# The last row of w_down in two loads, of 88 and of 40 partitions

## The chip, the cores and the metric

One core of a Trainium2 chip runs the kernel. The metric is device time in microseconds (us) of one execution. Most executions agree within 0.3%. With five or six executions the 95% intervals below reach about 0.13% to each side, which is 0.24 us, so a difference of 0.1 us can't be told from the times.

## The reference

A decode step for two rows: an adaLN modulation, an attention over a window of the key and value caches, and a gated feed-forward layer. Only its end matters here:

```python
def _B_ref(x, w_gate, w_up, w_down):
    return _gelu(x @ w_gate) * (x @ w_up) @ w_down
...
h = _layernorm(x, axis=-1) * (1 + cb) + sb
x = x + gb * _B_ref(h, B_w_gate, B_w_up, B_w_down)      # w_down is 1536 x 640, bf16
```

## The kernel before

The kernel is a stream of loads. One queue (SP) brings 77 MB of weights and caches into one large tile, `arena`; the engines work on each part as it lands. Each of the 128 partitions gets 12 consecutive rows of `w_down`, and these 12 "rows" (one row is 640 elements, 1280 B, in each partition) come in three loads: rows 0 to 7, rows 8 to 10, and row 11 alone. The last load is small so that little work is left when the last byte is in.

```python
WD_SPLIT = [(0, 8), (8, 3), (11, 1)]
...
sem_of = {it: S.sem("d_%s" % "_".join(str(z) for z in it)) for it in place}   # a semaphore for each load
...
        return B_w_down.rearrange("(p r) n -> p (r n)", r=FC)[:, r0 * D:(r0 + nr) * D]
...
def pump(*consumed):
    ...
        queue["ops"][it] = S.dma("sp", k_dma(view(it), source(it)), sem_of[it], writes=keys(it), ...)
...
for ci, (r0, nr) in enumerate(WD_SPLIT):
    def f(e, r0=r0, nr=nr):
        for fc in range(r0, r0 + nr):                 # four matmuls for each row
            wv = wd_v[:, fc, :].rearrange("p (i n) -> p i n", i=NR)
            for i in range(NR):
                last = e.matmul(ps[32 * i:32 * i + RM, BK_OT, CY:CY + DR], lhsT=aT[:, fc, :], rhs=wv[:, i, :], ...)
        return last
    S.op("pe", f, reads=["aT"] + keys(("wd", ci)), writes=[bank(BK_OT)], name="down%d" % ci)
# then two DVE operations (fin, finb) and the store of the result
```

A load's semaphore gets 16 increments in all. Where a load runs on 16 DMA engines, each engine adds one when its share has landed, so the landing of a load is the landing of its slowest engine.

## Time and profile before

| | before |
|---|---|
| time, median of 6 runs | 186.06 us (185.94 to 186.15) |
| share of 16 DMA engines' span filled by the SP queue | 96.9% |
| rows 0 to 7: landed, matmuls start | 180.52, 180.65 us |
| rows 8 to 10: landed, matmuls start | 181.65, 181.70 us |
| row 11: landed, matmuls start | 182.05, 182.09 us |

The landings are the last of a load's 16 semaphore increments in the trace; the matmul starts are from the timeline.

Part 3 of the page of the kernel before gives, for each DMA queue, its packets, the megabytes and the share of 16 engines' span that its packets took. The loads fill the machine.

```profile
q1 hardware_dynamic: 2604, 76.88, 96.9%
q8 instruction: 5, 0.08, 0.2%
```

The end of the chain of waits of the kernel before (start, duration, what; in us), followed back from the last instruction. The 26 us of DMA are not 26 us of work on w_down: the load was issued early and stood behind others. What it says is that the last matmuls wait for w_down.

```profile
155.58 26.07 DMA arena<-in_B_w_down_dram
181.65 0.04 issue
181.70 0.39 PE ps L706 x12
182.08 0.01 issue
182.09 0.28 PE ps L706 x4
182.37 0.02 issue
182.39 0.34 DVE fin L711
```

The timeline of the kernel before over the same stretch (start, duration, engine, line, operation, output and inputs, count, and in brackets the idle time ahead and what ended it). The three groups of weight loads (PEld) of line 706 are the three loads' rows: 32 matmuls, 12 and 4.

```profile
180.63 0.54 PEld L706 LDWEIGHTS ps<-arena,aT 128*17 128x17 bf16 x32 [0.38 <-DVE aT L697]
...
181.69 0.18 PEld L706 LDWEIGHTS ps<-arena,aT 128*17 128x17 bf16 x12 [0.52 <-DMA arena<-in_B_w_down_dram]
...
182.09 0.10 PEld L706 LDWEIGHTS ps<-arena,aT 128*17 128x17 bf16 x4 [0.21 <-DMA arena<-in_B_w_down_dram]
182.39 0.33 DVE L711 TENSOR_TENSOR fin<-ps,modR 128x160 f32<-128x160 f32 x1 [1.81 <-PE ps L706]
```

Quarter-microsecond windows of the kernel before. The columns after the window's length are the busy times of PE, PEld, DVE, ACT and POOL with counts, then PE's clock, the mean busy share of the 16 DMA engines, and GB/s. The share falls from 0.96 to 0.49 at 179.50 and then needs two microseconds to reach zero: the engines end one after another.

```profile
179.25:179.50 0.25, 0.11 (x2) 0.00 (x0) 0.01 (x1) 0.00 (x0) 0.00 (x0) 1.00 0.96 374
179.50:179.75 0.25, 0.00 (x0) 0.00 (x0) 0.25 (x1) 0.00 (x0) 0.00 (x0) 1.00 0.49 190
179.75:180.00 0.25, 0.00 (x0) 0.00 (x0) 0.25 (x1) 0.00 (x0) 0.00 (x0) 1.00 0.53 210
...
181.00:181.25 0.25, 0.25 (x24) 0.17 (x12) 0.00 (x0) 0.00 (x0) 0.00 (x0) 1.00 0.21 77
181.25:181.50 0.25, 0.14 (x8) 0.00 (x0) 0.00 (x0) 0.00 (x0) 0.00 (x0) 1.00 0.10 36
181.50:181.75 0.25, 0.05 (x4) 0.06 (x8) 0.00 (x0) 0.00 (x0) 0.00 (x0) 1.00 0.02 5
```

The trace also holds every DMA packet with its start, duration, size and queue, but not its engine, and no view prints them one by one. A packet starts where the one before it on its engine ends, so the packets can be chained into 16 engines. Where the text below speaks of an engine's packets, it is from such chains. The engine that ended last ran its last packet at 181.51 us; the first engine was done with everything at about 179.45. The five engines that end more than 1.4 us behind the first are the five that carried one packet of the instruction queue each (16 KB, 0.94 to 1.07 us long, at 36, 97, 135, 162 and 177 us). Each such packet left its engine about 1.5 us behind: about 1 us is the packet itself, and the data packet right behind it took about 0.5 us longer than others of its size (at 178 us, 880 ns where 385 is usual). Nothing later gave that back, since every engine has an equal share of every load. A sixth engine, with an 8 KB packet at 89 us, is 1.0 us behind. In what follows these six are the late engines.

### The profile page before, as it was taken

The page shows a single profiled execution, that of the slowest core. Times are in us where ns is not written, and L with a number is a line of the kernel's source. Part 1 is how long each engine was busy: PE and PEld are TensorE (multiplying, and loading weights), DVE is VectorE, ACT ScalarE, POOL GpSimd, SP SyncE. Part 2 cuts the span into 40 slices and gives each one's busy share as a digit, 9 for nine tenths or more (in the row PEclk, how much of TensorE's full clock was granted, in tenths as well). Part 3 has the DMA queues.
Part 4 walks back from the last instruction along what each step waited for, and adds up shares of the span by engine and source line. Part 5 has one row for each costly group of instructions (what it writes and reads, how often), then busy time and mean ns, then how long its engine had stood idle before and what let it go on. Part 6 is the DMA issues. An engine that isn't in the chain of part 4 may idle for free.

```text
span 184.9 us, 1610 instructions
## 1 busy us (share of the span) xinstructions
PE 104.3 (56%) x843; PEld 26.1 (14%) x552; DVE 106.8 (58%) x97; ACT 14.5 (8%) x28; POOL 6.7 (4%) x29
## 2 busy tenths in 40 slices
PE   0015400937666096662598667748663299866853
PEld 0011000020000000001360002400000266411211
DVE  6213000039996489965994999387995649302311
ACT  2032100060000000001000000100000100220410
POOL 7700000000000000000000000000000000000000
PEclk9999999996999759998599999987999669999999
DMA  9999998999897999999898989899999989899980
GB/s 349 433 495 425 425 425 362 429 425 495 367 511 340 511 404 447 457 394 479 374 479 365 500 351 500 383 468 436 425 450 394 491 367 486 378 388 435 419 365 28
DMA packets 2626, 76.97 MB, mean 416 GB/s; under 512 B 314, under 2 KB 444, under 8 KB 572
## 3 DMA queue, kind: packets, MB, share of 16 engines
q1 hardware_dynamic: 2604, 76.88, 96.9%
q8 instruction: 5, 0.08, 0.2%
q14 instruction: 1, 0.01, 0.0%
q10 hardware_dynamic: 16, 0.01, 0.0%
HBM read 76.88 MB, written 0.00 MB: 416 GB/s over the span
## 4 chain that ended last, share of the span: by engine, by line
DMA 57%; DVE 22%; PE 17%; ACT 1%; issue 1%; SPq 0%
DMA arena<-in_A_k_cache_dram 36%; DMA arena<-in_B_w_down_dram 14%; DVE arena L518 12%; DMA arena<-in_w_mod_dram 8%; PE ps L581 8%; DVE S_sb L537 6%; PE ps L530 5%; DVE Em L567 2%; PE ps L470 2%; DVE negm L547 1%; ACT E_sb L555 1%; PE ps L558 1%; DVE M L543 0%; PE ps L551 0%; SPq L287 0%
## 5 line engine op out<-in xcount | busy, mean ns | idle before, releaser
L530 PE MATMUL ps<-arena,ident_b 128*128 128x512 bf16 x192 | 50.7, 411 | 30.2 <-DVE arena L518 30.1
L518 DVE TENSOR_TENSOR arena<-arena,qbc 128x3072 bf16<-128x3072 bf16 x32 | 54.8, 1749 | 11.1 <-DMA arena<-in_A_k_cache_dram 11.1
L581 PE MATMUL ps<-arena,Em 128*64 128x384 bf16 x256 | 24.5, 357 | 5.6 <-DVE Em L567 5.6
L537 DVE TENSOR_REDUCE S_sb<-ps 128x32 f32<-128x1024 f32 x16 | 19.5, 1219 | 8.4 <-PE ps L530 8.4
L581 PEld LDWEIGHTS ps<-arena,Em 128*64 128x64 bf16 x256 | 15.4, 121 | 29.8 <-DVE Em L567 22.2
L567 DVE TENSOR_TENSOR Em<-E_sb,maskE 128x2048 bf16<-128x2048 bf16 x8 | 18.0, 2282 | 2.6 <-PE ps L581 2.6
L492 PE MATMUL ps<-arena,hT 128*2 128x512 bf16 x60 | 4.7, 485 | 11.7 <-DMA arena<-in_A_wq_dram 11.7
L502 DVE CAST qrow<-ps 128x512 bf16<-128x512 f32 x1 | 0.7, 693 | 15.6 <-PE ps L492 15.6
L545 PEld LDWEIGHTS ps<-ident_f,M 128*1 128x1 f32 x2 | 0.2, 80 | 61.5 <-DVE M L543 61.5
L555 ACT ACTIVATE E_sb<-S_sb,nbias 128x256 bf16<-128x256 f32 x2 | 1.0, 507 | 69.3 <-DVE nbias L553 69.3
L651 DVE COPY arena<-ps 128x320 f32<-128x320 f32 x1 | 0.5, 491 | 10.1 <-PE ps L643 10.1
L643 PE MATMUL ps<-arena,oT 128*2 128x320 bf16 x96 | 3.9, 299 | 2.4 <-DMA arena<-in_A_wo_dram 2.4
L588 ACT ACTIVATE On<-ps,rden 128x384 bf16<-128x384 f32 x2 | 1.2, 582 | 47.5 <-PE ps L581 47.5
L403 PE MATMUL ps<-ident_b,crow 2*128 2x2 bf16 x5 | 0.4, 177 | 7.9 <-POOL zsel L383 7.9
L678 PE MATMUL ps<-arena,h2T 128*2 128x384 bf16 x40 | 3.8, 455 | 1.7 <-DMA arena<-in_B_w_up_dram 1.4
L470 PE MATMUL ps<-arena,scT 128*17 128x480 bf16 x40 | 4.3, 597 | 0.5 <-DMA arena<-in_w_mod_dram 0.5
L415 PE MATMUL ps<-Em,ident_b 128*128 128x512 bf16 x17 | 4.2, 379 | 0.2 <-issue 0.2
L408 DVE CAST X<-xr 128x160 f32<-128x160 bf16 x1 | 0.2, 244 | 6.1 <-DMA xr<-in_A_x_dram 6.1
L687 DVE TENSOR_TENSOR aR<-ps,gl 128x384 bf16<-128x384 f32 x1 | 0.6, 558 | 5.4 <-PE ps L678 5.4
L424 PE MATMUL ps<-st,selstat 128*128 128x2 f32 x4 | 0.9, 298 | 4.9 <-ACT sqj L420 4.9
L478 DVE TENSOR_SCALAR opc<-modR 128x160 f32<-128x160 f32 x2 | 0.5, 245 | 5.1 <-ACT modR L475 5.1
L492 PEld LDWEIGHTS ps<-arena,hT 128*2 128x2 bf16 x20 | 0.6, 100 | 15.8 <-issue 15.8
(89 smaller groups left out, 52.6 us busy)
## 6 DMA issues: line engine op xcount, KB each, us to landing
arena<-in_A_v_cache_dram SPq DMA_DIRECT2D x4, 6144.0 KB, 27.2
arena<-in_A_k_cache_dram SPq DMA_DIRECT2D x3, 6144.0 KB, 36.0
arena<-in_A_wq_dram SPq DMA_DIRECT2D x1, 7680.0 KB, 31.3
arena<-in_A_wo_dram SPq DMA_DIRECT2D x1, 6240.0 KB, 27.0
arena<-in_A_k_cache_dram SPq DMA_DIRECT2D x2, 3072.0 KB, 42.7
arena<-in_w_mod_dram SPq DMA_DIRECT2D x1, 4800.0 KB, 14.0
arena<-in_B_w_gate_dram SPq DMA_DIRECT2D x1, 1920.0 KB, 20.7
arena<-in_B_w_up_dram SPq DMA_DIRECT2D x1, 1920.0 KB, 22.7
```

Source lines behind the costliest of these rows:

```text
L415: last = e.matmul(ps[:, BK_T, :], lhsT=ident_b[:, :], rhs=Em[:, 0, 0:512 // H, :].rearrange("p j h -> p (j h)"), start=True, stop=True)
L470: last = e.matmul(ps[32 * i:32 * i + RM, half, 0:MH].rearrange("p (m n) -> p m n", n=DR), lhsT=scT[:, k, :], rhs=wv[:, 3 * half:3 * half + ...
L492: last = e.matmul(ps[32 * i:32 * i + B, n, :], lhsT=hT[:, k, :], rhs=wv[:, kk, i, n * QW:(n + 1) * QW], start=(k == 0), stop=(k == KT - 1) ...
L518: S.op("dve", lambda e: e.tensor_tensor(out=kt, in0=kt, in1=qbc[:, b, :].unsqueeze(1).broadcast_to([P, JC, Dh]), op=ALU.mult), reads=[("qb ...
L530: last = e.matmul(o_ap, lhsT=ident_b[:, :], rhs=kt[:, :, t * GC:(t + 1) * GC], start=(t == 0), stop=(t == NCH - 1))
L537: S.op("dve", lambda e: e.tensor_reduce(out=S_sb[:, b, 2 * JC * pair:2 * JC * (pair + 1)], in_=ps[:, 2 * z:2 * z + 2, :].rearrange("p k (j ...
L547: S.op("dve", lambda e: e.tensor_reduce(out=negm[:, b, :].rearrange("p (h x) -> p h x", x=XQ), in_=ps[0:1, BK_T, 0:P].rearrange("p (h x) - ...
L555: S.op("act", lambda e: e.activation(out=E_sb[:, b, :], in_=S_sb[:, b, :], func=ACTF.Exp, scale=SCALE, bias=nbias[:, b:b + 1], accum_out=d ...
L567: S.op("dve", lambda e, z=z, j=j: e.tensor_tensor(out=Em[:, z, :, :], in0=E_sb[:, b, j:j + JE].unsqueeze(2).broadcast_to([P, JE, H]), in1= ...
L581: last = e.matmul(ps[64 * i:64 * i + 2 * H, BK_O, 0:ON], lhsT=Em[:, z, 2 * jp:2 * jp + 2, :].rearrange("p j h -> p (j h)"), rhs=view(it, l ...
L643: last = e.matmul(ps[32 * i:32 * i + B, bk, 0:w], lhsT=oT[:, t, :], rhs=wv[:, tl, lo:lo + w], start=(t < NR), stop=(t >= NT - NR), tile_po ...
L678: last = e.matmul(ps[32 * i:32 * i + B, bk, 0:FT].rearrange("p (m r) -> p m r", r=FR), lhsT=h2T[:, k, :], rhs=wk[:, i, :, :], start=(k == ...
```

## The change

The intent: row 11 should not be put on the engines that end late. A load of 88 partitions and a load of 40 partitions use 11 and 10 of the 16 DMA engines, so that five engines carry nothing of the last row. Each of the two loads has its own semaphore, and the last four matmuls wait for both.

```diff
         sem_c = S.sem("d_c")
-        sem_of = {it: S.sem("d_%s" % "_".join(str(z) for z in it)) for it in place}
+        LAST = ("wd", len(WD_SPLIT) - 1)
+        LAST_SPLIT = [(0, 88), (88, P)]
+        sem_of = {it: S.sem("d_%s" % "_".join(str(z) for z in it)) for it in place if it != LAST}
+        sem_last = [S.sem("d_last%d" % n) for n in range(len(LAST_SPLIT))]
...
-                queue["ops"][it] = S.dma("sp", k_dma(view(it), source(it)), sem_of[it], writes=keys(it), ...)
+                if it == LAST:
+                    for n, (p0, p1) in enumerate(LAST_SPLIT):
+                        S.dma("sp", k_dma(view(it)[p0:p1, :], source(it)[p0:p1, :]), sem_last[n], writes=keys(it) if n == 0 else [("last", n)], ...)
+                else:
+                    queue["ops"][it] = S.dma("sp", k_dma(view(it), source(it)), sem_of[it], writes=keys(it), ...)
...
-            S.op("pe", f, reads=["aT"] + keys(("wd", ci)), writes=[bank(BK_OT)], name="down%d" % ci)
+            S.op("pe", f, reads=["aT"] + keys(("wd", ci)) + ([("last", n) for n in range(1, len(LAST_SPLIT))] if ("wd", ci) == LAST else []), ...)
```

More of the change, by code (lines that the diff above doesn't have):

```diff
@@ L336, in pump @@
                     break
-                queue["ops"][it] = S.dma("sp", k_dma(view(it), source(it)), sem_of[it], writes=keys(it), name="ld_%s" % "_".join(str(z) for z in it))
+                if it == LAST:
+                    for n, (p0, p1) in enumerate(LAST_SPLIT):
+                        S.dma("sp", k_dma(view(it)[p0:p1, :], source(it)[p0:p1, :]), sem_last[n], writes=keys(it) if n == 0 else [("last", n)], name="ld_last%d" % n)
+                else:
+                    queue["ops"][it] = S.dma("sp", k_dma(view(it), source(it)), sem_of[it], writes=keys(it), name="ld_%s" % "_".join(str(z) for z in it))
                 queue["next"] += 1
@@ L708, in f @@
                 return last
-            S.op("pe", f, reads=["aT"] + keys(("wd", ci)), writes=[bank(BK_OT)], name="down%d" % ci)
+            S.op("pe", f, reads=["aT"] + keys(("wd", ci)) + ([("last", n) for n in range(1, len(LAST_SPLIT))] if ("wd", ci) == LAST else []), writes=[bank(BK_OT)], name="down%d" % ci)
         S.op("dve", lambda e: e.tensor_tensor(out=fin[:, :], in0=ps[:, BK_OT, CY:CY + DR], in1=modR[:, 5, :], op=ALU.mult),
```

## The prediction

> **What bounds the kernel now.** Its loads: the page's third part has the SP queue's packets filling 96.9% of 16 engines' span. The chain of waits is 57% DMA; its last stretch is 26.07 us of w_down loading (155.58 to 181.65), then the final matmuls, two DVE operations and the store. The last row (160 KB) is the last load.
>
> **How the loads end.** In quarter-microsecond windows the DMA share is about 0.96 until 179.50, then 0.49, 0.53, 0.40, 0.36, 0.33, 0.29, 0.21, 0.10, 0.02: the engines do not end together. I chained the trace's packet records end to start. The fastest engine ends the last row at 179.45, eleven engines within 1.0 us of it, five at +1.5 to +2.1 us, the slowest at 181.56. Each of the five carried one 16 KB instruction fetch (at 36, 97, 135, 162, 177 us), which put it about 1.5 us behind. This gives no engine numbers. Each engine carries 8 packets of the last row, one every 52 ns: 0.41 us.
>
> **What the last row costs.** In the timeline the matmuls of rows 0 to 7 start at 180.65, those of rows 8 to 10 at 181.70 (load landed 181.66), those of row 11 at 182.09 (landed 182.05). A row takes four matmuls, 0.07 us, so row 11 could have issued at about 181.92. Its own exposed wait is only 0.17 us. Rows 8 to 10 arrive as late as before on the slowest engine; that 0.5 us wait isn't touched.
>
> **What the change does.** The Trainium skill, "DMA: Bandwidth & Descriptors", section "Why a DMA increments its semaphore by 16 and not by 1", says the engine count is the largest number up to 16 that divides the outer dimension, and that the lowest-numbered engines are used; no run here shows it yet. Then engines 0 to 9 carry 8 + 4 packets (0.62 us, +0.21), engine 10 carries 8, engines 11 to 15 none. It adds one issue on SP (0.44 us, 26 us early: free) and a second semaphore ahead of row 11's matmuls (the same double wait takes a 51 ns instruction at 180.54; hidden if both landed).
>
> - The five late engines are 11 to 15, as the choice of 88 and 40 suggests: the last row lands near 181.2, before rows 8 to 10; row 11 follows at once: -0.12 to -0.17 us. Chance 0.6.
> - The slowest is skipped but another late one isn't: landing near 182.05, nothing won, perhaps +0.05. 0.2.
> - The slowest is among 0 to 9: landing at 182.26, +0.2 to +0.3 us. 0.2.
>
> **Predicted time:** 185.93 us, range 185.75 to 186.30. Faster by over 2%: 0.003; within 2%: 0.994; slower by over 2%: 0.003. The change touches at most the 0.4 us between 181.70 and 182.09, 0.2% of the time.
>
> **What would show it right.** In the timeline the 16 matmuls of rows 8 to 11 run as one burst from about 181.70 with no wait ahead of row 11; the final multiplication on DVE starts at about 182.22 instead of 182.39; in the packet records five engines show no 1280 B packets at the end and ten show twelve. Wrong: row 11's wait for DMA as long or longer, with a late engine showing twelve packets.
>
> **What would make it wrong.** Late engines with low numbers; fetches on other engines in another build; another split of 88 and 40 over engines; a shift of the load of rows 8 to 10.

## The result

| | before | after |
|---|---|---|
| time, median of 6 runs each | 186.06 us | 186.47 us (186.25 to 186.61) |
| ratio after to before | | 1.0021, 95% interval 1.0008 to 1.0034 |
| rows 0 to 7: landed | 180.52 us | 180.58 us |
| rows 8 to 10: landed, matmuls start | 181.65, 181.70 us | 181.91, 181.96 us |
| row 11: landed, matmuls start | 182.05, 182.09 us | 182.19 (88) and 182.36 (40), 182.50 us |
| last packet of the last row starts | 181.51 us | 181.71 us |

A ratio is the mean time of one kernel's runs over that of the other's of the same rounds, so it is not quite the ratio of the medians quoted beside it. By the 2% bound the two kernels are the same; the difference of about 0.4 us is nevertheless clear of the noise, and it is a loss.

Part 3 of the page after: five packets more (two loads have 21 completions instead of 16), the same bytes.

```profile
q1 hardware_dynamic: 2609, 76.88, 96.8%
```

The end of the chain of waits after. It now comes from the second load of row 11, and "issue" between its landing and the matmuls is 0.14 us where it was 0.04.

```profile
156.15 26.21 DMA arena<-in_B_w_down_dram
182.36 0.14 issue
182.50 0.27 PE ps L713 x4
182.77 0.02 issue
182.79 0.34 DVE fin L718
```

The timeline after. Row 11's wait is longer (0.33 us idle, 0.21 before), and the wait of rows 8 to 10, which the change was not to touch, is longer too (0.72, before 0.52).

```profile
180.68 0.56 PEld L713 LDWEIGHTS ps<-arena,aT 128*17 128x17 bf16 x32 [0.57 <-DVE aT L704]
...
181.96 0.18 PEld L713 LDWEIGHTS ps<-arena,aT 128*17 128x17 bf16 x12 [0.72 <-DMA arena<-in_B_w_down_dram]
...
182.47 0.13 PEld L713 LDWEIGHTS ps<-arena,aT 128*17 128x17 bf16 x4 [0.33 <-DMA arena<-in_B_w_down_dram]
182.50 0.25 PE L713 MATMUL ps<-arena,aT 128*17 128x160 bf16 x4 [0.15 <-DMA arena<-in_B_w_down_dram]
182.79 0.32 DVE L718 TENSOR_TENSOR fin<-ps,modR 128x160 f32<-128x160 f32 x1 [2.35 <-PE ps L713]
```

The windows after. Look at the last two columns together: between 179.50 and 180.00 the engines are some 40% busier than before (0.71 and 0.73 against 0.49 and 0.53) and move only some 10% more (236 and 210 GB/s against 190 and 210). The packets take longer. The engines then also end later.

```profile
179.25:179.50 0.25, 0.00 (x0) 0.00 (x0) 0.16 (x1) 0.00 (x0) 0.00 (x0) 1.00 0.86 328
179.50:179.75 0.25, 0.00 (x0) 0.00 (x0) 0.25 (x1) 0.00 (x0) 0.00 (x0) 1.00 0.71 236
179.75:180.00 0.25, 0.04 (x1) 0.04 (x2) 0.15 (x1) 0.00 (x0) 0.00 (x0) 1.00 0.73 210
...
181.00:181.25 0.25, 0.25 (x28) 0.24 (x16) 0.00 (x0) 0.00 (x0) 0.00 (x0) 1.00 0.35 118
181.25:181.50 0.25, 0.20 (x12) 0.00 (x0) 0.00 (x0) 0.00 (x0) 0.00 (x0) 1.00 0.25 87
181.50:181.75 0.25, 0.00 (x0) 0.00 (x0) 0.00 (x0) 0.00 (x0) 0.00 (x0) 1.00 0.08 26
```

The packets say it more sharply. Rows 8 to 10 are 128 packets of 3840 B. Before, they all took 149 to 160 ns, and all 128 packets of row 11 took 55 ns. After, 26 of the 3840 B packets took over 165 ns, up to 261, and 27 of row 11's took over 63 ns, up to 89. All of this "stretch" lies between about 179.4 us and the end.

The chains also show who carried the last row after the change: ten engines with 12 packets, one with 8, five with none. The five with none were four early engines and one late one (fetch at 36 us); the engine with 8 was late (fetch at 177 us); the other four late engines carried 12.

### The profile page after: what moved, and what is told of

The parts are those of the page before. It is cut to its first block, busy times and chain, and to the rows that moved or that the text cites. A ratio compares the mean times of both kernels' runs of the same rounds, so it can differ in the third digit from the quotient of the medians.

```text
span 185.3 us, 1612 instructions
## 1 busy us (share of the span) xinstructions
PE 105.4 (57%) x843; PEld 26.9 (15%) x552; DVE 106.7 (58%) x97; ACT 14.5 (8%) x28; POOL 6.7 (4%) x29
## 4 chain that ended last, share of the span: by engine, by line
DMA 57%; DVE 22%; PE 17%; ACT 1%; SPq 1%; issue 1%
DMA arena<-in_A_k_cache_dram 35%; DMA arena<-in_B_w_down_dram 14%; DVE arena L525 12%; PE ps L588 8%; DMA arena<-in_w_mod_dram 8%; DVE S_sb L544 6%; PE ps L537 5%; DVE Em L574 2%; PE ps L477 2%; SPq L290 1%; DVE negm L554 1%; ACT E_sb L562 1%; PE ps L565 1%; PE ps L558 1%; DVE M L550 0%
## 5 line engine op out<-in xcount | busy, mean ns | idle before, releaser
L537 PE MATMUL ps<-arena,ident_b 128*128 128x512 bf16 x192 | 49.3, 400 | 28.4 <-DVE arena L525 28.3
L588 PE MATMUL ps<-arena,Em 128*64 128x384 bf16 x256 | 25.5, 368 | 5.7 <-DVE Em L574 5.7
L588 PEld LDWEIGHTS ps<-arena,Em 128*64 128x64 bf16 x256 | 15.9, 124 | 30.4 <-DVE Em L574 22.2
L499 PE MATMUL ps<-arena,hT 128*2 128x512 bf16 x60 | 6.0, 583 | 11.8 <-DMA arena<-in_A_wq_dram 11.8
```

The lines of the kernel that those rows point to most:

```text
L499: last = e.matmul(ps[32 * i:32 * i + B, n, :], lhsT=hT[:, k, :], rhs=wv[:, kk, i, n * QW:(n + 1) * QW], start=(k == 0), stop=(k == KT - 1) ...
L537: last = e.matmul(o_ap, lhsT=ident_b[:, :], rhs=kt[:, :, t * GC:(t + 1) * GC], start=(t == 0), stop=(t == NCH - 1))
L588: last = e.matmul(ps[64 * i:64 * i + 2 * H, BK_O, 0:ON], lhsT=Em[:, z, 2 * jp:2 * jp + 2, :].rearrange("p j h -> p (j h)"), rhs=view(it, l ...
```

## The experiments

The theories at the start. A: the late engines carry more, and the second wait costs a little. B: having two loads at all costs it. All edits are shown against the changed kernel ("after"); "one semaphore" is always the same edit. The table has all runs; "stretched" counts the 3840 B packets of rows 8 to 10 that took over 165 ns, of 128, and the longest of them.

| run | row 11 comes as | semaphores | median us (runs) | ratio to before, 95% interval | stretched, longest ns |
|---|---|---|---|---|---|
| before | 128 partitions | 1 | 186.02 to 186.09 in each but one | 1 | 0, 160 |
| after | 88, 40 | 2 | 186.47 (6) | 1.0021 (1.0008 to 1.0034) | 26, 261 |
| after_again | 88, 40 | 2 | 186.54 (5) | 1.0026 (1.0013 to 1.0038) | 20, 407 |
| one_sem | 88, 40 | 1 | 186.36 (5) | 1.0017 (1.0004 to 1.0030) | 27, 262 |
| two_64 | 64, 64 | 2 | 186.41 (6) | 1.0021 (1.0009 to 1.0033) | 24, 273 |
| two_64_one_sem | 64, 64 | 1 | 186.42 (5) | 1.0020 (1.0008 to 1.0033) | 23, 266 |
| four_32_one_sem | 32 four times | 1 | 186.95 (5) | 1.0046 (1.0032 to 1.0060) | 35, 241 |
| cols_two_sem | 128, by columns, twice | 2 | 186.20 (5) | 1.0009 (0.9996 to 1.0021) | 0, 156 |
| cols_one_sem | 128, by columns, twice | 1 | 186.11 (5) | 1.0000 (0.9987 to 1.0012) | 0, 158 |
| even_odd | 64 even, 64 odd | 1 | 185.90 (5) | 0.9996 (0.9982 to 1.0010) | 0, 160 |
| even_odd_60 | 60 even, 60 odd, 8 | 1 | 186.45 (5) | 1.0020 (1.0006 to 1.0034) | 27, 244 |
| other_source (wrong result) | 64, 56, 8 from w_gate | 1 | 186.33 (2) | 1.0013 (0.9984 to 1.0042) | 27, 227 |
| crossed_read (wrong result) | 128, rows permuted | 1 | 186.49 (2) | 1.0022 (0.9993 to 1.0051) | 25, 246 |
| into_lower (wrong result) | 64, 56, 8 into 0 to 63 | 1 | 186.57 (1) | one run | 25, 279 |
| into_upper (wrong result) | 64, 56, 8 into 64 to 127 | 1 | 186.53 (1) | one run | 29, 295 |
| staircase | 16, 15, ... 5, 2 | 1 | 188.14 (1) | one run | 30, 229 |
| into_first16 (wrong result) | 16, 15, ... 5, 2 into 0 to 15 | 1 | 188.18 (1) | one run | 24, 407 |

(Into_lower and into_upper had one execution of the kernel before, 185.79 us. Two entries of the last column hold something else besides: in after_again and into_first16 an instruction fetch ended at about 179.1 to 179.3 us, and the two packets right behind it, of 407 and 352 and of 407 and 382 ns, took 0.46 and 0.49 us more than 149 ns each would be, about the delay that follows every fetch. Without them the counts are 18 and 22, the longest 234 and 308 ns.)

### The change once more

> The changed kernel once more, as the yardstick for the others of this call on the same chip: 186.3 to 186.6 us, that is +0.3 to +0.5 us on the kernel before. If it were within 0.1 us of the kernel before, the measured loss would belong to the first chip or build and not to the change.

Measured: 186.54 us, ratio 1.0026. The loss belongs to the change. In this run's trace the chains place the fetches otherwise than in the first: three of the five late engines carried nothing of the last row, one carried 8 and one 12 packets. The time was no better for it.

### One semaphore

```diff
-        sem_last = [S.sem("d_last%d" % n) for n in range(len(LAST_SPLIT))]
+        sem_last = [S.sem("d_last")] * len(LAST_SPLIT)
```

> Both loads of the changed kernel count on one semaphore, so the row-11 matmuls have one wait instead of two; the loads and engines stay. Theory A (part of the loss is the second wait: in the changed kernel row 11 started 0.11 to 0.14 us after its load had landed, before 0.04 us): 0.07 to 0.12 us faster than the changed kernel, so about +0.3 us on the kernel before. Theory B (the loss is only in the loads): no difference, within 0.05 us, from the changed kernel.

Measured: 186.36 us against 186.54, ratios 1.0017 and 1.0026, whose intervals overlap. The times lean to theory A and do not settle it. The traces are steadier. From the last landing to the first weight load of row 11 the four traces with two semaphores (the changed kernel twice, two_64, cols_two_sem) all show 0.104 us, and those with one show 0.041 or 0.042. So the second wait costs 0.06 us there, and some 0.03 us more until the first matmul. It is a small part of the loss.

### Two equal loads

```diff
-        LAST_SPLIT = [(0, 88), (88, P)]
+        LAST_SPLIT = [(0, 64), (64, P)]
```

> The last row in two loads of 64 and 64 partitions, 16 engines each by the divisor rule, so every engine carries 4 + 4 packets as in the one load before; two loads and two waits stay. If the loss comes from the late engines' carrying 12 packets instead of 8 (and from what that disturbs): +0.05 to +0.15 us on the kernel before, from the second wait alone. If it comes from having two loads at all (one more issue, one more completion on each engine): +0.3 us or more, as the changed kernel.

Measured: 186.41 us, ratio 1.0021. Every engine carried 8 packets of row 11, as before the change, and still the loss was there. The 12 packets on late engines can thus not be what the loss consists of. The timeline of this run shows what the change shows: rows 8 to 10 come late.

```profile
182.06 0.18 PEld L713 LDWEIGHTS ps<-arena,aT 128*17 128x17 bf16 x12 [0.70 <-DMA arena<-in_B_w_down_dram]
...
182.47 0.13 PEld L713 LDWEIGHTS ps<-arena,aT 128*17 128x17 bf16 x4 [0.23 <-DMA arena<-in_B_w_down_dram]
```

24 packets of 3840 B were stretched. The late engines' lag behind the first engine grew by 0.30 to 0.33 us over rows 0 to 10 (leaving out the engine whose fetch, at 177 us, falls into that stretch); before, it did not grow at all (by 0.00 to 0.01 us).

### A census of engine numbers

```diff
-        LAST_SPLIT = [(0, 88), (88, P)]
+        LAST_K = list(range(16, 4, -1)) + [2]
+        LAST_SPLIT = [(sum(LAST_K[:n]), sum(LAST_K[:n + 1])) for n in range(len(LAST_K))]
... and one semaphore
```

> A census of engine numbers, not a candidate: the last row in 13 loads of 16, 15, 14 ... 5 and 2 partitions, one packet for each engine used, one semaphore. If the divisor rule and the lowest-numbered rule hold, engine 15 carries 1 packet of 1280 B, 14 carries 2, ... 5 carries 11, engines 2 to 4 carry 12, engines 0 and 1 carry 13, so the packet records name the late engines. My theory of why the prediction failed: at least three of the five engines that carried a 16 KB instruction fetch have numbers 0 to 10 (the rival, that they are 11 to 15 and the loss has another cause, would show the five late chains with 1 to 5 packets). Time: an engine with 13 loads has 13 completions; landing some 0.3 to 0.5 us later than before, 186.3 to 186.8 us.

Measured: the five fetch engines carried 10, 11, 2, 7 and 6 packets (fetches at 37, 95, 133, 162 and 177 us). By the rule these are engines 6, 5, 14, 9 and 10. (Among the early engines, which run side by side, one packet of the count was put on the wrong chain; the late ones stand apart.) The later run into_first16 gave the same five numbers, in another order: 14, 5, 6, 9, 10. The coarser marks of the first run of the change, of one_sem, into_lower, into_upper, other_source and even_odd_60 all fit these five numbers. Only after_again does not, though it is the same program as the first run and ran on the same chip as one_sem and the staircase. So the choice of 88 and 40 mostly skips one late engine of five, number 14.

The time, 188.14 us, was beyond the 186.3 to 186.8 expected. The last packet began at 181.81 us, as late as in the others, but the last landing came at 184.01: the last ten increments arrive over 0.91 us. The two late engines that have 10 and 11 completions to deliver would then need about 0.2 us for each (an estimate from these increments). Completions close behind one another on one engine are not free.

### By columns, with two semaphores and with one

```diff
-        LAST_SPLIT = [(0, 88), (88, P)]
+        LAST_SPLIT = [(0, D // 2), (D // 2, D)]
...
-    S.dma("sp", k_dma(view(it)[p0:p1, :], source(it)[p0:p1, :]), sem_last[n], ...)
+    S.dma("sp", k_dma(view(it)[:, p0:p1], source(it)[:, p0:p1]), sem_last[n], ...)
```

> The last row in two loads again, two semaphores, but cut by columns: each load has all 128 partitions and 320 of the 640 columns, so each engine writes the same partitions as in the one load before. Theory P (cutting by partitions makes engines that are done write into partitions that a late engine is still writing, and both slow down): no stretched packets, 3840 B packets stay at 149 to 160 ns where the two loads of 64 showed up to 273 ns; +0.05 to +0.2 us on the kernel before, from the second wait and the smaller packets. Theory L (any second load costs it): +0.35 us or more, stretched packets as with 64 and 64.

> The same column cut with one semaphore, hence one wait. Theory P: within 0.1 us of the kernel before, and 0.05 to 0.12 us faster than the column cut with two semaphores. Theory L: +0.25 us or more on the kernel before.

Measured: 186.20 and 186.11 us, ratios 1.0009 and 1.0000. No packet was stretched: the 3840 B packets took 149 to 158 ns, and all 256 packets of 640 B took 32 ns. Theory L falls: a second load by itself costs nothing that the times show, and the second wait (0.1 us at most) is within their noise. The timeline of the version with one semaphore is that of the kernel before, to 0.05 us:

```profile
180.65 0.53 PEld L713 LDWEIGHTS ps<-arena,aT 128*17 128x17 bf16 x32 [0.38 <-DVE aT L704]
...
181.72 0.18 PEld L713 LDWEIGHTS ps<-arena,aT 128*17 128x17 bf16 x12 [0.54 <-DMA arena<-in_B_w_down_dram]
...
182.14 0.10 PEld L713 LDWEIGHTS ps<-arena,aT 128*17 128x17 bf16 x4 [0.24 <-DMA arena<-in_B_w_down_dram]
```

So of the two cuts it is the one by partitions that costs. The Trainium skill, "DMA: Bandwidth & Descriptors", section "Rules for kernel authors", says of two transfers to disjoint partition halves: "Don't bother". This agrees, with +0.35 to +0.39 us for two halves by the medians.

### Two halves on one semaphore, and four quarters

```diff
-        LAST_SPLIT = [(0, 88), (88, P)]
+        LAST_SPLIT = [(0, 64), (64, P)]                              # two_64_one_sem
+        LAST_SPLIT = [(32 * n, 32 * n + 32) for n in range(4)]       # four_32_one_sem
... and one semaphore
```

> Two loads of 64 partitions on one semaphore. Theory P: the stretched packets stay (3840 B packets of 200 ns and more between 179.5 and 180.5 us), the late engines' lag grows by 0.2 to 0.3 us across the rows 0 to 10, and the time is +0.25 to +0.35 us on the kernel before, the second wait's 0.1 us less than with two semaphores. If the whole loss were the second wait: within 0.1 us of the kernel before.

> Four loads of 32 partitions, 2 packets on each of 16 engines, one semaphore. Theory P: what slows a late engine is the 8 packets that others write into its partitions, and those are as many as with two loads of 64, so about +0.3 us again, at most +0.1 more for the two extra completions on each engine. Theory L: the loss grows with the number of loads, +0.6 us or more.

Measured: two halves 186.42 us, +0.35 by the medians, as theory P expected, though no better than with two semaphores. Four quarters 186.95 us, +0.88, which is theory L's number and not theory P's. But the trace of the four quarters has about as much stretch as the others, and its last packet began at 181.69. Its last landing came 0.87 us after that, where the kernel before has 0.54 and the runs with two loads 0.42 to 0.65: four completions, 2 packets apart, seem to wait for each other as in the staircase. (The profiled execution, 186.69 us, was the shortest of the five, so the trace shows less of the loss than the median.) Theory P stands, with this second cost beside it for short loads.

### Where the stretch comes from: the half that is written

```diff
+        LAST_SPLIT = [(0, 64), (64, 120), (120, P)]                  # one semaphore
+        scratch = sb("scratch", [P, D], BF16)
...
+    # into_lower: destination of load n
+    (view(it)[p0:p1, :] if n == 0 else scratch[p0 - 64:p1 - 64, :])
+    # into_upper
+    (scratch[p0 + 64:p1 + 64, :] if n == 0 else view(it)[p0:p1, :])
```

> Wrong result on purpose: the 128 rows of the last load are read as before, in loads of 64, 56 and 8 partitions (16, 14 and 8 engines, so the packet counts 9, 8 and 4 mark engines 0 to 7, 8 to 13 and 14 to 15), but all are written into partitions 0 to 63, rows 64 to 127 into a spare tile. Theory P, with the Trainium skill's map (a load of 128 partitions is written by engines 0 to 7 into partitions 0 to 63 and by 8 to 15 into 64 to 127): the 3840 B packets of rows 8 to 10 on engines 0 to 7 that still run after 179.4 us are stretched, to 180 ns and more in the mean, those on engines 8 to 15 stay at 149 to 160 ns. Theory H (the slowing is on the side that reads memory, which this leaves as it was): stretched on late engines of both halves.

> The mirror image, also wrong on purpose: all 128 rows are written into partitions 64 to 127. Theory P: the 3840 B packets on late engines 8 to 15 are stretched, those on engines 0 to 7 stay at 149 to 160 ns. Theory H: stretched on late engines of both halves, as when written into the lower half.

The map is in the Trainium skill, "DMA: Bandwidth & Descriptors", section "The descriptor swizzle". Measured, mean of the 3840 B packets after 179.3 us on the engines with fetches: into_lower 214 and 202 ns on engines 0 to 7, and 194, 180 and 191 ns on engines 8 to 15. Into_upper 200 and 180 ns on 0 to 7, and 182, 187 and 203 ns on 8 to 15. Both halves are stretched in both runs. That a late engine is slowed only by writes into its own partitions, as theory P had it, is refuted, if the map holds. Theory H, the reading side, was left.

### The reading side

```diff
+    # other_source: LAST_SPLIT as above, right destinations, one semaphore
+    k_dma(view(it)[p0:p1, :], source(("wg", 0))[p0:p1, 0:D])
+    # crossed_read: one load
+    k_dma(view(it), B_w_down.rearrange("(j i r) n -> i j r n", i=16, r=FC)[:, :, FC - 1, :])
```

> Wrong result on purpose: the last row's loads (64, 56 and 8 partitions, the right destinations, one semaphore) read 1280 B from each row of w_gate, which was loaded long before, instead of w_down's last row; row step and sizes are the same. Theory H (two engines that read the same 15 KB row of w_down at one time slow each other): the stretch goes: the 3840 B packets on late engines stay under 165 ns in the mean and their lag grows by under 0.1 us over rows 0 to 10. Theory S (it comes from writing: engines crossing each other's partitions, or the fabric backed up): stretched as in the two runs before, 180 to 215 ns in the mean and 0.3 us of lag.

> Wrong result on purpose: one load of 128 partitions as in the kernel before, but partition 8i+j gets the last row of w_down's partition 16j+i, so each engine reads rows that belong to others while it writes (by the 128-partition map) only its own partitions. Theory H: late engines' 3840 B packets stretched, 180 ns and more in the mean, and the time +0.2 to +0.4 us on the kernel before. Theory S: no stretch (under 160 ns), within 0.15 us of the kernel before, if writing is still split as for other loads of 128 partitions, which the record doesn't show.

Measured: reading another tensor left the stretch in place (27 packets; means on the fetch engines 185, 185, 171, 166 and 159 ns, a little less than the 180 to 214 of the two runs before; lag +0.2 to +0.3 us). Theory H falls as it was put: that two engines read the same rows at one time is not it. A cause on the reading side is not thereby ruled out: these loads, too, change which engine reads which rows, and no run here changes the split of the writing alone. The single load with permuted rows was stretched too, which looks like theory H, but its own text left a door open: the source now has 16 as its outer size, and the split of the writing may have changed with it. That run alone tells nothing.

### Even and odd partitions

```diff
+        LAST_SPLIT = [(0, 2), (1, 2)]                                 # even_odd, one semaphore
+    k_dma(view(it)[p0:P:p1, :], source(it)[p0:P:p1, :])
+        LAST_SPLIT = [(8, 2), (9, 2), (0, 1)]                         # even_odd_60, one semaphore
+    k_dma(view(it)[p0:P if p0 else 8:p1, :], source(it)[p0:P if p0 else 8:p1, :])
```

> A correct kernel: the last row in two loads of 64 partitions, the even ones and the odd ones, one semaphore, so each load reaches over all of the partitions' range instead of one half. If the stretch comes from engines' writing into partitions that another engine is writing (theory S, crossing), it stays: 3840 B packets on late engines 180 ns and more in the mean, +0.25 to +0.4 us on the kernel before. If it comes from 64 neighbouring partitions' taking only half of the write paths (theory S, narrow load), it shrinks by half or more: +0.0 to +0.2 us.

> A correct kernel: the last row in loads of the 60 even partitions from 8, the 60 odd ones from 9 (15 engines each by the divisor rule) and the first 8 (8 engines), one semaphore. Like the even and odd loads of 64 that lost nothing, the two large loads spread over the whole range, but 60 in 15 shares cannot line up with the shares of 8 that the loads of 128 have. If loads that reach only part of the range are what holds the engines up: no stretch (late 3840 B packets under 160 ns in the mean), within 0.15 us of the kernel before (the third completion may cost some). If engines' crossing into partitions of others is: 175 ns and more in the mean, +0.25 us or more.

Measured: the even and odd 64 lose nothing (185.90 us, ratio 0.9996, no packet stretched, row 11's packets 55 to 60 ns). The even and odd 60 lose 0.36 us by the medians (186.45, ratio 1.0020), with 27 stretched packets and means of 167 to 182 ns on the fetch engines, close to the 175 that was named. Their chains have 9, 8 and 0 packets on 8, 7 and 1 engines: 60 partitions do run on 15 engines. The large loads of these two runs lie almost on the same partitions; what differs most is whether the shares can line up with the shares of a load of 128, and the stretch follows that. The third load, 8 neighbouring partitions with one packet on each of 8 engines, differs too, and no run leaves it out. That the shares of the even and odd 64 do line up is inferred, since no record gives a packet's partition.

The timelines of the two, even_odd first. Only rows 8 to 10 and row 11 are shown.

```profile
181.73 0.18 PEld L713 LDWEIGHTS ps<-arena,aT 128*17 128x17 bf16 x12 [0.55 <-DMA arena<-in_B_w_down_dram]
...
182.13 0.10 PEld L713 LDWEIGHTS ps<-arena,aT 128*17 128x17 bf16 x4 [0.22 <-DMA arena<-in_B_w_down_dram]
```

Then even_odd_60:

```profile
181.91 0.18 PEld L713 LDWEIGHTS ps<-arena,aT 128*17 128x17 bf16 x12 [0.54 <-DMA arena<-in_B_w_down_dram]
...
182.26 0.10 PEld L713 LDWEIGHTS ps<-arena,aT 128*17 128x17 bf16 x4 [0.17 <-DMA arena<-in_B_w_down_dram]
```

### All into the first 16 partitions

```diff
+    # the staircase's 13 loads, issued once the tile's earlier part is free
+    k_dma(arena[0:p1 - p0, 8192 + n * D:8192 + n * D + D], source(it)[p0:p1, :])
```

> Wrong result on purpose: the staircase's 13 loads (engine numbers can be read off the packet counts) all write into partitions 0 to 15, into a free part of the same tile. If what a late engine suffers is others' writing into its own partitions (by the Trainium skill's map of a 128-partition load, engines 0 to 3 own partitions 0 to 15), late engines 4 to 15 keep 3840 B packets of 149 to 165 ns in the mean and any late engine 0 to 3 is stretched beyond 200. If busy write paths hold up every engine, late engines of all numbers are stretched, more than in the first staircase, as 128 packets now go to 16 partitions.

Measured: the fetch engines 6, 10, 14, 5 and 9 were all stretched (means 209, 226, 197, 190 and 173 ns), though by the map only engines 0 to 3 own partitions 0 to 15. So, if the map holds, engines that are not the target are held up too. (The 226 includes the packet of 382 ns behind a fetch; without it the mean is 199.) In the first staircase, with the right destinations, the means are 168 to 181 ns: more stretch with the narrower destination, as the second alternative expected, in single executions.

The Trainium skill, "DMA: Bandwidth & Descriptors", section "Back-pressure in remote DMA", says that a saturated destination port backs up to the engines that share the way to it. It says so of transfers between cores. It would fit a hold-up of engines that do not write there, but no run here shows the ports, and this stays a guess.

## Why the prediction was wrong

**What held.** The bound, the place (what differs in the matmuls lies between 180.5 and 182.5 us), no change beyond 2%, and the split. Whether 0.17 us could have been won was not tested, since no run skipped all the late engines. The Trainium skill's rule for the engine count ("DMA: Bandwidth & Descriptors", "Why a DMA increments its semaphore by 16 and not by 1") agrees with the trace: the semaphore of the load of 88 has one early update, at 156.23 us, and then 11 as the data lands, so the early one must bring the five missing increments; that of the load of 40 has one at 156.62 us and then 10. That the engines used are the lowest-numbered is the page's word; the counts of 12, 8 and 0 packets show only that the 10 engines of one load are among the 11 of the other.

**The step that failed first** is the case that was given a chance of 0.6: "The five late engines are 11 to 15, as the choice of 88 and 40 suggests". It was read out of the change's shape and not out of a record. By the packet counts of the two staircases and that page's rule they are engines 5, 6, 9, 10 and 14, in all readable runs but one. Only one of five is skipped.

**The case that came true had the wrong size.** In the first run of the change the engine farthest behind just ahead of the last row was skipped and another late one was not. For this the prediction had "landing near 182.05, nothing won, perhaps +0.05". The landing was at 182.36 and the matmuls began 0.41 us later than before. In the two profiled runs the sum is: the last packet starts 0.20 us later; from it to the last landing 0.65 us instead of 0.54, +0.11; from the landing to the weight load 0.104 instead of 0.041, +0.06; from there to the first matmul +0.03. Without stretch the engine that ended last (1.81 us behind the first, which ended rows 8 to 10 at 179.15) would have ended row 11 at 179.15 + 1.81 + 0.62 = 181.58, about when the slowest engine did before (181.57). It ended at 181.76. The 0.11 us is not shown to belong to the change: one_sem, with the same loads, has 0.50 us there. One pair of traces is also a matter of chance: in the trace of cols_two_sem, without any stretch, the last packet began at 181.87 because its slowest engine was 2.4 us behind. That the loss is the change's rests on the medians.

**The term left out is the stretch,** and it, not the wrong engine numbers, accounts for the loss: two_64, which keeps no engine free of the last row, loses as much, and by the estimate above the last row would otherwise have ended about when it did before. The prediction treated the 16 engines as independent: packets keep their 52 ns, and rows 8 to 10 arrive "as late as before on the slowest engine; that 0.5 us wait isn't touched". They arrived 0.26 us later. With the last row cut by partitions into neighbouring pieces, packets of early and late engines alike took longer. In the two loads of 64 every engine has 8 packets, as before the change. So the loss is a loss of the cut: what the 11 and 10 engines win or lose on top of it can't be seen in the times.

**The second wait** was called hidden "if both landed". The second load is the last to land, so it never is: 0.06 us, or 0.09 us to the first matmul.

**What stays open.** Why packets are stretched on engines whose partitions nobody else writes, and whether it happens at the SBUF ports or ahead of them. That shares which do not line up with those of the loads of 128 are the trigger fits the runs (halves, quarters, 88 and 40, 60 even and odd, the staircases stretched; columns, 64 even and odd, one plain load of 128 not). But which partitions an engine writes or reads in those loads is not on record, and crossed_read, one load of 128 that was stretched, fits only if its writing was split otherwise. So the trigger is inferred, and whether the reading or the writing causes the stretch is open. Also open is why the fetches fell on other engines in one run. No version here beats the kernel before: even_odd at 0.9996 is the same within its interval.

## What to carry to other kernels

Cut a load by columns, or leave it whole: a cut into neighbouring partitions changes which engine reads and writes what, and at the end of this stream, where some engines were still busy with earlier loads, packets of early and late engines took longer, and the loss of 0.4 us was more than the whole prize, 0.17 us by the prediction's estimate. Before steering work away from late DMA engines, find out which numbers they have with loads of 16, 15, 14 ... partitions, and why they are late; here the cause is the program's own instruction fetches. Two loads that one consumer waits for should count on one semaphore, with a wait for the full count of both (0.09 us in the traces, too little for the times to show), and short loads in a row pay for each completion.

## What the Trainium skill lacked or had wrong

- "DMA: Bandwidth & Descriptors", "Rules for kernel authors", gives as the reason against disjoint partition halves that they share the same 16 engines. It lacks that they also slow packets of other loads in flight: 3840 B packets of 149 ns took up to 273 ns beside two loads of 64 partitions, and 149 to 158 ns beside two loads cut by columns. It also lacks that 64 even and 64 odd partitions cost nothing (0.9996) while 60 and 60 do (1.0020).
- The same page, "Latency and other measured facts", names engines 7 and 15 as usually slower, and limits its best guess at the cause to DMAs issued from GpSimd (the software path). These loads come from the SP queue, so the page is not contradicted. Here the late ones are 5, 6, 9, 10 and 14 by their packet counts in all readable runs but one. No page says that an instruction fetch (16 KB, 0.94 to 1.07 us) leaves one engine of a saturated stream about 1.5 us behind until the end, some 0.5 us of it on the data packet behind the fetch (880 ns instead of 385).
- The same page, "Why a DMA increments its semaphore by 16 and not by 1": the count rule agrees (11, 10 and 15 engines for 88, 40 and 60 partitions). For loads from the SP queue the page does not give the cost of completions in close order: with 13 short loads the last landing came 2.2 us after the last packet began, with one load 0.54 us.
- "Back-pressure in remote DMA" speaks of transfers between cores only; into_first16 shows engines held up within one core, up to 308 ns for a packet of 149 ns, from whatever cause (leaving out two packets right behind a fetch).
- None of these pages has the price of a second semaphore wait ahead of a matmul: 0.104 us from landing to weight load with two semaphores, 0.041 us with one.
